# First theta stage and v's scales in another order: small operations first, an earlier table load, one sum on VectorE, mixing steps moved to the last slot

## The chip, the core and the metric

The kernel runs on one core of one Trainium2 chip. The metric is the device time of one execution in microseconds; runs are compared by their median, and one execution was taken by the hardware profiler. Times in the trace count from the start of that execution's span.

## What is computed

Windowed attention for 8 batches of 8 heads, then a block that rotates, mixes tokens and mixes channels. The reference, cut to the formulas:

```python
scores = scale * np.matmul(q, k.transpose(0, 1, 3, 2))        # 8 x 8 x 576 x 576, head size 64
mask = (rel >= 0) & (rel < 128)
scores = np.where(mask, scores + bias[None], -1e9)
attn = softmax(scores)                                        # with 1e-9 added to the sum
x = np.matmul(attn, v)                                        # to (batch, 576, 512)
theta = x @ w_theta
zr, zi = x * np.cos(theta), x * np.sin(theta)
y = einsum('ts,bsd->btd', w_tok_r, zr) + einsum('ts,bsd->btd', w_tok_i, zi)
u = x + y
return u + np.maximum(u @ w_ch, 0.0)
```

## The kernel before

The 576 tokens are five tiles, four of 128 and one of 64. Heads go in pairs, four pairs a batch. For a pair, TensorE makes the scores from `qh` and `kh` (and, from the seventh pair on, the low parts `ql` and `kl`), VectorE adds the bias and takes the row's least value (`weigh`, L552), ScalarE takes the exp (L555) into `front` and `back`. The weights are transposed, on TensorE for the early pairs (copied back as `pt`, L575), and by a DMA for the later ones, from `hl`: a cast by ScalarE (L580) and its remainder by VectorE (L583). `values` multiplies by v, `finish` (L614 to L621) writes `x_sb`.

The theta stage (`turn`) of a batch flips `x_sb` block by block on TensorE (`columns`, L655). ScalarE casts a block to `x_hi` (L665 for the short first one, L673), VectorE makes the remainder (L667, L674: `x_lo`). `products` multiplies by `wth_hi` and `wth_lo`, 8 or 12 matmuls a block; `angle` and `waves` reduce the angle and take sine and cosine on ScalarE, which needs another function table (L741 loads it); `turned` multiplies by x and the scale `zs` (L721 on VectorE) and splits the result into two f16 halves, `z_hi` (L647, ScalarE) and `z_lo` (L649, VectorE; L727 and L728 for the short block). `mix` is token mixing: nine chunks c for eight groups of outputs, three matmuls a step, with `z_hi`, `z_hi` and `z_lo`; L810 to L815 finish a group. Mixing of batch 0 is a generator whose steps are handed out while batch 1's attention runs: FIRST gives four counts for each pair.

Everything is in f16 or f32r halves with power-of-two scales, and these must be known first. In the first theta stage `scales_from` takes the largest sum over rows (`sums`, by L216 on ScalarE while the token weights are unpacked by L196, L197, L203 and L206) and over columns (`add_sizes`: TensorE sums |w| with a column of ones), `spread_from` (L315) flips and reduces a peak over partitions, and `scales_to` spreads it and makes `zs`. For v, `add_up` (L309) sums |v| over three groups of heads on ScalarE (L312), `spread_first` and `spread_scales` make its scale for batch 1's later pairs. The channel weights are unpacked one after the other (`late`, with L203, L206, L211, L212) during batch 1's attention.

The source order, `issue_after` and `high_priority` feed a scheduler that lists each engine's instructions once, before the run; each engine works through its list in order and waits at semaphores. From the first mixing matmul on, TensorE keeps the source order.

```python
FIRST = ((9, 2, 1, 7), (3, 3, 4, 3), (4, 3, 4, 2), (3, 3, 3, 0))
KEPT = 3                     # token-weight chunks that are split late: wtk_lo by L235
GROUP = 4                    # heads whose v is loaded and measured together
```

## Time and profile before

| | us |
|---|---|
| median of 3 runs (lowest, highest) | 625.47 (623.98, 626.39) |
| profiled execution | 623.47 |
| its span, first to last instruction | 621.7 |
| TensorE busy | 595.0 (96%) |
| VectorE busy | 522.5 (84%) |
| ScalarE busy | 486.6 (78%) |
| GpSimd busy | 207.9 (33%) |

In the rows, PE is TensorE's matmuls and PEld its weight loads, DVE is VectorE, ACT ScalarE, POOL GpSimd, SPq SyncE's queue of DMA issues; L12 is line 12 of the kernel before. A tile's name stands without its buffer's number. Idle time in brackets is the time just before an instruction in which its engine did nothing, with what ended it. Busy time on an engine that waits for others elsewhere says little by itself: the stage and the wait that ends last there count.

### The profile page before, as it was taken

The numbers are of one execution on the slowest core, as the hardware profiler recorded it, in microseconds if no ns is written. First come the engines' busy times: TensorE is split into PE (matmuls) and PEld (weight loads), VectorE is DVE, ScalarE is ACT, GpSimd is POOL, SyncE is SP. The second block draws the span as 40 slices with busy tenths as digits, with TensorE's granted clock in tenths as the row PEclk, the third lists the DMA queues.
The fourth block names the chain that finished last, engine by engine and source line by source line (L and its number), as shares of the span: only waits on it lengthen the run. The fifth ranks groups of instructions, "written<-read, shape, count | busy, mean of one in ns | idle before, by whom it ended". The sixth has DMA issues, their size and how long they took to land.

```text
span 621.7 us, 14873 instructions
## 1 busy us (share of the span) xinstructions
PE 595.0 (96%) x5731; PEld 488.6 (79%) x5731; DVE 522.5 (84%) x1345; ACT 486.6 (78%) x918; POOL 207.9 (33%) x261
## 2 busy tenths in 40 slices
PE   4997899889999999999999999999999999999997
PEld 3796678767888888888778878887888878887776
DVE  4889796989999889998899889997899879946733
ACT  3988899878788689887998699877998798828610
POOL 5963304440325312541225312441235221530200
PEclk9899999989999999999999999999999999999999
DMA  8971112791268901984079902994089703650001
GB/s 315 390 250 45 35 35 88 177 219 38 77 155 189 216 30 52 212 212 103 30 143 196 221 30 60 211 210 107 20 182 177 157 30 86 103 98 29 21 20 58
DMA packets 137847, 78.10 MB, mean 126 GB/s; under 512 B 110768, under 2 KB 127280, under 8 KB 137776
## 3 DMA queue, kind: packets, MB, share of 16 engines
q1 hardware_dynamic: 137776, 77.15, 51.6%
q8 instruction: 45, 0.74, 0.5%
q14 instruction: 26, 0.21, 0.1%
HBM read 40.44 MB, written 9.44 MB: 80 GB/s over the span
## 4 chain that ended last, share of the span: by engine, by line
PE 48%; DVE 26%; ACT 19%; DMA 3%; issue 3%; SPq 0%; DVEq 0%; ACTq 0%
PE mm L77 38%; PE ps L77 8%; DVE hl L583 3%; ACT front L555 2%; DVE back L552 2%; ACT back L555 2%; DVE z_lo L649 2%; DVE g L721 2%; DVE front L552 2%; PE ps L102 2%; ACT z_hi L647 1%; ACT g L712 1%; DVE f L721 1%; DVE f L702 1%; ACT g L705 1%
## 5 line engine op out<-in xcount | busy, mean ns | idle before, releaser
L77 PE MATMUL mm<-wtk_hi,z_lo 128*128 128x288 f16 x576 | 165.4, 287 | 0.7 <-DVE z_lo L649 0.6
L77 PE MATMUL mm<-wtk_hi,z_hi 128*128 128x288 f16 x576 | 165.8, 288 | 0.0
L77 PE MATMUL mm<-wtk_lo,z_hi 128*128 128x288 f16 x576 | 165.4, 287 | 0.0
L77 PEld LDWEIGHTS <-z_hi 128*128 128x128 f16 x1152 | 109.1, 98 | 29.9 <-issue 0.3
L814 POOL TENSOR_SCALAR us<-xtf,fixed 128x288 f32<-128x288 f32 x56 | 79.1, 1416 | 84.9 <-DVE xtf L810 83.4
L77 PE MATMUL mm<-u,wch_hi 128*128 128x288 f16 x512 | 81.3, 286 | 0.0
L555 ACT ACTIVATE front<-front,fixed 128x256 f32<-128x256 f32 (+2 forms) x160 | 60.1, 443 | 15.3 <-DVE fixed L552 15.1
L77 PEld LDWEIGHTS <-z_lo 128*128 128x128 f16 x576 | 56.6, 98 | 15.9 <-DVE z_lo L649 1.3
L77 PEld LDWEIGHTS <-wch_hi 128*128 128x128 f16 x512 | 48.1, 98 | 18.2 <-issue 7.1
L812 ACT ACTIVATE u<-xtf,fixed 128x288 f16<-128x288 f32 x64 | 33.5, 526 | 32.7 <-DVE xtf L810 32.6
L555 ACT ACTIVATE back<-back,fixed 128x256 f32<-128x256 f32 x128 | 56.3, 494 | 2.4 <-DVE fixed L552 2.4
L815 POOL TENSOR_TENSOR u<-us,u 128x288 f16<-128x288 f32 x56 | 41.4, 754 | 46.2 <-DVE vl L486 30.5
L649 POOL TENSOR_TENSOR z_lo<-g,z_hi 128x512 f16<-128x512 f32 x14 | 16.4, 1170 | 107.5 <-ACT z_hi L647 107.5
L77 PE MATMUL ps<-vh,pt 128*128 128x65 f16 x936 | 47.4, 194 | 3.3 <-DMA pt<-hl 3.3
L77 PE MATMUL ps<-kh,qh 64*128 64x256 f32 (+1 forms) x304 | 46.5, 344 | 4.0 <-DVE x_sb L621 2.0
L77 PEld LDWEIGHTS <-pt 128*128 128x128 f16 x1404 | 46.3, 98 | 5.0 <-DMA pt<-hl 3.8
L77 PE MATMUL mm<-wth_hi,x_hi 128*128 128x512 f32 x160 | 46.6, 413 | 2.6 <-DVE x_hi L667 2.6
L77 PE MATMUL ps<-vl,pt 128*128 128x64 f16 x468 | 45.6, 193 | 0.0
L810 DVE SCALAR_TENSOR_TENSOR xtf<-mm,fixed,xtf 128x288 f32<-128x288 f32 x64 | 32.1, 510 | 15.0 <-PE mm L77 15.0
L77 PE MATMUL mm<-wth_lo,x_hi 128*128 128x512 f32 x160 | 44.0, 395 | 0.0
L843 DVE SCALAR_TENSOR_TENSOR xtf<-mm,fixed,xtf 128x288 f32<-128x288 f32 x64 | 32.8, 513 | 12.4 <-PE mm L77 11.0
L77 PE MATMUL mm<-u,wch_lo 128*128 128x288 f16 x256 | 41.8, 286 | 0.0
(215 smaller groups left out, 1439.4 us busy)
## 6 DMA issues: line engine op xcount, KB each, us to landing
vb<-in_vx_dram SPq DMA_DIRECT2D x16, 650.0 KB, 5.3
out_dram<-xtf SPq DMA_DIRECT2D x64, 144.0 KB, 1.7
qr<-in_qk_dram SPq DMA_DIRECT2D x26, 320.0 KB, 3.1
kr<-in_qk_dram SPq DMA_DIRECT2D x26, 288.0 KB, 4.2
xtf<-in_wch_dram SPq DMA_DIRECT2D x4, 512.0 KB, 3.5
qh<-in_qk_dram SPq DMA_DIRECT2D x6, 320.0 KB, 6.1
kh<-in_qk_dram SPq DMA_DIRECT2D x6, 288.0 KB, 6.4
xtf<-in_wtok_dram SPq DMA_DIRECT2D x3, 576.0 KB, 9.8
```

The lines of the kernel that those rows point to most:

```text
L77: ins = nc.tensor.matmul(*args, **kw)
L102: ins = nc.tensor.transpose(*args)
L552: self.weighed = nc.vector.tensor_tensor_reduce(out=sb, in0=ps, in1=bias, scale=self.scale, scalar=3.0e38, op0=ALU.add, op1=ALU.min, accum ...
L555: self.exps.append(nc.scalar.activation(sb, sb, AF.Exp, bias=least, scale=-1.0))
L583: self.lowered = nc.vector.scalar_tensor_tensor(out=hl[:, 1], in0=src, scalar=2.0 ** PEXP, in1=hl[:, 0], op0=ALU.mult, op1=ALU.subtract)
L649: low = engine.tensor_tensor(out=z_lo[:, c, :], in0=z, in1=z_hi[:, c, :], op=ALU.subtract)
L721: nc.vector.scalar_tensor_tensor(out=z, in0=x_sb[:, i, :], scalar=zs[:, c:c + 1], in1=z, op0=ALU.mult, op1=ALU.mult)
L810: nc.vector.scalar_tensor_tensor(out=xtf[:, m, cs], in0=y_ps[:, :HALF], scalar=st["back"], in1=xtf[:, m, cs], op0=ALU.mult, op1=ALU.add)
L812: nc.scalar.activation(u_hi[:, m, cs], xtf[:, m, cs], AF.Copy, scale=up)
L814: nc.gpsimd.tensor_scalar(out=us[:, m, cs], in0=xtf[:, m, cs], scalar1=up, scalar2=None, op0=ALU.mult)
L815: lows.append(lambda m=m, cs=cs: nc.gpsimd.tensor_tensor(out=u_lo[:, m, cs], in0=us[:, m, cs], in1=u_hi[:, m, cs], op=ALU.subtract))
L843: nc.vector.scalar_tensor_tensor(out=xtf[:, e, cs], in0=o_ps[:, :HALF], scalar=down, in1=xtf[:, e, cs], op0=ALU.mult, op1=ALU.max)
```

## The change

In the first theta stage `add_sizes` gets a first matmul with a small constant (`least`), which stands for the 1.0 that L423 added; the sums of the second half are made before the second block's products; the three parts of the scale chain are placed between the products of blocks 1, 2 and 3 in the source (`late`, `place`), and `x_lo`, L725 and L726 come after the bound. The table load (`early`) waits for the attention's exps and `x_hi` alone. The last token weights are unpacked in another order (`lift`, HOLD), and the three late splits follow the bound. `turned` runs for four blocks at once (`j >= 3`). For v, `largest` takes the third group's largest |v| on VectorE in place of a sum on ScalarE, `spread_first` and `spread_scales` stand half a pair earlier. FIRST gives the first pair two steps less and the last pair five more; three fewer run after it.

```diff
-FIRST = ((9, 2, 1, 7), (3, 3, 4, 3), (4, 3, 4, 2), (3, 3, 3, 0))
+HOLD = 2
+
+FIRST = ((9, 2, 1, 5), (3, 3, 4, 3), (4, 3, 4, 2), (3, 4, 7, 0))
...
+        def lift(k, t):
+            if k in lifted:
+                return
+            lifted.append(k)
+            _, z, b = words(k, t)
+            nc.vector.scalar_tensor_tensor(out=b, in0=z, scalar=3, in1=b, op0=ALU.logical_shift_left,
+                                           op1=ALU.bitwise_or)
+
         def together(k, t):
             raw, z, b = words(k, t)
             val = b.bitcast(F32)
-            nc.vector.scalar_tensor_tensor(out=b, in0=z, scalar=3, in1=b, op0=ALU.logical_shift_left,
-                                           op1=ALU.bitwise_or)
+            lift(k, t)
...
-            for stage, fn in ((3, split), (2, together), (1, apart)):
+            for stage, fn in ((3, split), (2, together), (1, apart)) if k != n else ((1, apart), (2, together)):
                 j = k - stage
+                if j == n - 2 and stage == 2:
+                    lift(j, tiles[j])
+                    yield HOLD
                 if 0 <= j < n and (stage < 3 or j < n - KEPT):
                     if j not in tiles:
                         tiles[j] = load(j)
                     fn(j, tiles[j])
                     if stage == 3:
                         del tiles[j]
-                    if stage == 1 and j > 0:
+                    if k == n and stage == 2:
+                        row(j)
+                    elif stage == 1 and 0 < j < n - 1:
                         row(j - 1)
...
+    def largest(g, to):
+
+        nc.vector.tensor_reduce(out=to, in_=group_v[g].rearrange("p h c d -> p (h c) d")[:, :, :64],
+                                axis=mybir.AxisListType.XY, op=ALU.max, apply_absolute_value=True)
...
         if start:
             size_ps.append(ps_m.tile([128, 512], F32, name="mm")[:, :HALF])
+            mm(size_ps[hf], one.broadcast_to([128, 128]), least.broadcast_to([128, HALF]), start=True, stop=False)
         for c in some:
-            mm(size_ps[hf], one.broadcast_to([128, 128]), sizes[c][:, hf * HALF:hf * HALF + HALF],
-               start=(start and c == some[0]), stop=(stop and c == some[-1]))
+            mm(size_ps[hf], one.broadcast_to([128, 128]), sizes[c][:, hf * HALF:hf * HALF + HALF], start=False,
+               stop=(stop and c == some[-1]))
...
                                 op0=ALU.mult, op1=ALU.max)
-        add_sizes(1, ORDER[:7], True, False)
         for hf in range(2):
-            add_sizes(hf, ORDER[7:], False, True)
+            add_sizes(hf, ORDER[8:], False, True)
             nc.vector.tensor_reduce(out=lim if hf else peak[:, 3:4], in_=size_ps[hf], axis=mybir.AxisListType.X,
                                     op=ALU.max)
-        nc.vector.tensor_scalar(out=peak[:, 3:4], in0=peak[:, 3:4], scalar1=lim, scalar2=2.0 ** (WEXP - 1),
-                                op0=ALU.max, op1=ALU.mult)
-        nc.vector.tensor_scalar(out=peak[:, 3:4], in0=peak[:, 3:4], scalar1=1.0, scalar2=None, op0=ALU.add)
+        return nc.vector.tensor_scalar(out=peak[:, 3:4], in0=peak[:, 3:4], scalar1=lim, scalar2=2.0 ** (WEXP - 1),
+                                       op0=ALU.max, op1=ALU.mult)
...
+            with tc.issue_after(st["bound"].ins) if "bound" in st else nullcontext():
+                st["rest"] = nc.vector.tensor_tensor(out=x_lo, in0=x_ps, in1=x_hi.bitcast(F32), op=ALU.subtract)
...
-        def products(t_ps, x_hi, x_lo):
+        def products(t_ps, x_hi, x_lo, late=None):
             prods = ((x_hi, wth_hi), (x_hi, wth_lo)) + (((x_lo, wth_hi),) if x_lo is not None else ())
             for k, (a, w) in enumerate(prods):
                 for c in range(4):
+                    if late is not None and (k, c) == late[0]:
+                        late[1]()
...
+                with nullcontext() if st["b"] else tc.issue_after(st["bound"].ins):
+                    nc.vector.tensor_tensor(out=g[:64], in0=x_sb[:64, i, :], in1=g[:64], op=ALU.mult)
+                    nc.vector.tensor_tensor(out=g[64:], in0=x_sb[:64, i, :], in1=f[:64], op=ALU.mult)
...
-            if not st["b"]:
-                early(st["exps"] + [st["kept"], row_sums[-1]])
...
                 if not st["b"] and j == 0:
+                    early(st["exps"] + [st["lifted"]])
                     with tc.issue_after(st["flipped"].ins):
                         add_sizes(0, ORDER[:7], True, False)
                 for k, g in enumerate(coming(st["b"])):
                     if j == k and st["b"]:
                         with tc.issue_after(st["rest"].ins):
                             measure(g, peaks[st["b"] % 2][:, GROUP * k:GROUP * k + GROUP])
-                ready.append(theta(i, cur))
+                def between_products():
+                    with tc.issue_after(st["angled"].ins), tc.high_priority(FINISH):
+                        if j == 1:
+                            st["bound"] = scales_from()
+                        elif j == 2:
+                            st["diag"] = spread_from(peaks[0], 4, "0")
+                        else:
+                            scales_to(st["diag"])
+
+                place = {1: (2, 0), 2: (1, 0), 3: (1, 0)}.get(j) if not st["b"] else None
+                ready.append(theta(i, cur, place and (place, between_products)))
                 if st["b"] != 1:
                     waves(*ready[-1])
                 elif j > 2:
                     for some in ready:
                         waves(*some)
-                if j < 3 and not st["b"]:
+                if j == 0 and not st["b"]:
                     with tc.issue_after(st["angled"].ins), tc.high_priority(FINISH):
-                        if j == 0:
-                            scales_from()
-                        elif j == 1:
-                            diag = spread_from(peaks[0], 4, "0")
-                        else:
-                            scales_to(diag)
-                if j >= (2, 3, 0)[min(st["b"], 2)]:
+                        add_sizes(1, ORDER[:8], True, False)
+                        add_sizes(0, ORDER[7:8], False, False)
+                if j >= (3, 3, 0)[min(st["b"], 2)]:
                     for some in ready:
                         turned(*some)
...
             step(mixing, steps[1])
-            if g == (b == 1):
+            if g == 0 and b > 1:
                 diag = spread_first(b - 1)
+            if b == 1 and g == 1:
+                spread_scales(0, diag)
             step(mixing, steps[2])
+            if b == 1 and g == 0:
+                with tc.issue_after(new.weighed.ins):
+                    largest(2, peaks[0][:, 2:3])
             pair.values()
             with tc.high_priority(FINISH):
                 done = pair.finish(x_sb)
-                if b == 1 and g == 1:
-                    spread_scales(0, diag)
             if new is not None and (new.early or g == 0):
...
                     with behind_all(new.exps):
-                        for k, g_v in enumerate(coming(0)):
+                        for k, g_v in enumerate(coming(0)[:2]):
                             add_up(g_v, peaks[0][:, k:k + 1])
...
 
     def start(x_sb, load):
...
-            with behind_all([st[0]["split"], st[0]["kept"]]):
+            with behind_all([st[0]["split"]]), tc.high_priority(FINISH):
                 while next(kept, False):
...
-    with tc.issue_after(done.ins):
-        for _ in kept:
-            pass
+    for k in range(KEPT):
+        with behind_all([done, st[0]["bound"]]):
+            next(kept, None)
...
-                    step(mixing, 6)
+                    step(mixing, 3)
```

Where it moves instructions, first on VectorE at the beginning of the first theta stage, from the end of the first batch's attention on. Before:

```order
L621 TENSOR_TENSOR x_sb<-ps,fixed 128x2x5x64
L203 SCALAR_TENSOR_TENSOR us<-us 128x576
L203 SCALAR_TENSOR_TENSOR xtf<-xtf 128x576
L235 SCALAR_TENSOR_TENSOR wtk_lo<-u,fixed,wtk_hi 128x576
L206 SCALAR_TENSOR_TENSOR us<-us 128x576
L667 TENSOR_TENSOR x_hi<-ps,x_hi 128x4x64
L206 SCALAR_TENSOR_TENSOR xtf<-xtf 128x576
L674 TENSOR_TENSOR x_lo<-ps,x_hi 128x512
```

With the change, whose lines are numbered anew (L209 was L203, L217 was L206, L246 was L235, L687 was L667, L695 was L674):

```order
L641 TENSOR_TENSOR x_sb<-ps,fixed 128x2x5x64
L209 SCALAR_TENSOR_TENSOR us<-us 128x576
L687 TENSOR_TENSOR x_hi<-ps,x_hi 128x4x64
L217 SCALAR_TENSOR_TENSOR us<-us 128x576
L209 SCALAR_TENSOR_TENSOR xtf<-xtf 128x576
L695 TENSOR_TENSOR x_lo<-ps,x_hi 128x512
L217 SCALAR_TENSOR_TENSOR xtf<-xtf 128x576
```

The low half of `x_hi` stands behind one of the four unpacking operations; the L235 of `u` comes some fifteen instructions later.

Then VectorE where z is made, at the end of the same stage. Before:

```order
L721 SCALAR_TENSOR_TENSOR g<-x_sb,fixed,g 128x512
L721 SCALAR_TENSOR_TENSOR f<-x_sb,fixed,f 128x512
L721 SCALAR_TENSOR_TENSOR wch<-x_sb,fixed,wch 128x512 x2
L728 SCALAR_TENSOR_TENSOR z_lo<-g,fixed,z_hi 128x512
L702 SCALAR_TENSOR_TENSOR wch<-wch,mm 128x512
L649 TENSOR_TENSOR z_lo<-g,z_hi 128x512
L649 TENSOR_TENSOR z_lo<-f,z_hi 128x512
L649 TENSOR_TENSOR z_lo<-wch,z_hi 128x512 x2
L702 SCALAR_TENSOR_TENSOR wch_lo<-wch_lo,mm 128x512
L721 SCALAR_TENSOR_TENSOR wch<-x_sb,fixed,wch 128x512 x2
L649 TENSOR_TENSOR z_lo<-wch,z_hi 128x512
L721 SCALAR_TENSOR_TENSOR wch_lo<-x_sb,fixed,wch_lo 128x512 x2
```

With the change (L745 was L721, L753 was L728, L726 was L702, L669 was L649):

```order
L745 SCALAR_TENSOR_TENSOR g<-x_sb,fixed,g 128x512
L745 SCALAR_TENSOR_TENSOR f<-x_sb,fixed,f 128x512
L745 SCALAR_TENSOR_TENSOR wch<-x_sb,fixed,wch 128x512 x2
L753 SCALAR_TENSOR_TENSOR z_lo<-g,fixed,z_hi 128x512
L745 SCALAR_TENSOR_TENSOR wch<-x_sb,fixed,wch 128x512 x2
L726 SCALAR_TENSOR_TENSOR wch_lo<-wch_lo,mm 128x512
L669 TENSOR_TENSOR z_lo<-g,z_hi 128x512
L669 TENSOR_TENSOR z_lo<-f,z_hi 128x512
L669 TENSOR_TENSOR z_lo<-wch,z_hi 128x512 x4
L745 SCALAR_TENSOR_TENSOR wch_lo<-x_sb,fixed,wch_lo 128x512 x2
L669 TENSOR_TENSOR z_lo<-wch_lo,z_hi 128x512 x2
```

The multiplications of all blocks but the last now stand ahead of the first remainder `z_lo`.

Last, ScalarE at the end of batch 1's attention, up to the second theta stage. Before:

```order
L484 ACTIVATE vh<-vb,fixed 128x5x64
L812 ACTIVATE u<-xtf,fixed 128x288
L580 ACTIVATE hl<-back 128x1024
L484 ACTIVATE vh<-vb,fixed 128x5x64
L456 ACTIVATE qh<-qr 128x640
L457 CAST kh<-kr 128x576
L665 CAST x_hi<-ps 128x4x64
L673 CAST x_hi<-ps 128x512
L812 ACTIVATE u<-xtf,fixed 128x288
```

With the change (L842 was L812, L600 was L580, L476 and L477 were L456 and L457, L504 was L484, L685 and L693 were L665 and L673):

```order
L842 ACTIVATE u<-xtf,fixed 128x288
L600 ACTIVATE hl<-back 128x1024
L476 ACTIVATE qh<-qr 128x640
L504 ACTIVATE vh<-vb,fixed 128x5x64
L477 CAST kh<-kr 128x576
L504 ACTIVATE vh<-vb,fixed 128x5x64
L842 ACTIVATE u<-xtf,fixed 128x288
L685 CAST x_hi<-ps 128x4x64
L693 CAST x_hi<-ps 128x512
```

One `vh` and one `u` now stand between `kh` and `x_hi`.

## Rows read from the trace of the kernel before

**Rows 1.** Busy time by stage: us, busy (instructions) of each engine, TensorE's clock, DMA.
```profile
107.00:122.00 15.00, 13.28 (x124) 11.61 (x122) 14.89 (x49) 12.61 (x28) 7.26 (x10) 1.00 0.78 190
...
140.00:152.00 12.00, 11.53 (x58) 9.52 (x59) 11.25 (x20) 10.09 (x16) 1.39 (x4) 1.00 0.20 46
```
**Rows 2.** TensorE's timeline: start us, us, instruction, idle time before and its end.
```profile
61.75 1.21 PE L77 MATMUL mm<-wth_hi,x_hi 128*128 128x512 f32 x4 [1.44 <-DVE x_hi L667]
...
70.85 0.30 PE L102 MATMUL mm<-fixed,peak 128*128 128x128 f32 x1 [1.91 <-ACT xtf L676]
...
81.50 0.30 PE L77 MATMUL mm<-wtk_hi,z_lo 128*128 128x288 f16 x1 [0.65 <-DVE z_lo L649]
...
105.47 0.39 PE L77 MATMUL ps<-kh,qh 64*128 64x256 f32 x2 [0.80 <-ACT pt L575]
...
114.92 0.38 PE L77 MATMUL mm<-fixed 128*128 128x3 f32 x2 [1.72 <-DVE fixed L321]
...
130.70 0.20 PE L77 MATMUL ps<-vh,pt 128*128 128x65 f16 x1 [0.51 <-DMA pt<-hl]
...
133.10 0.20 PE L77 MATMUL ps<-vh,pt 128*128 128x65 f16 x1 [1.87 <-DMA pt<-hl]
...
140.47 1.20 PE L77 MATMUL mm<-wth_hi,x_hi 128*128 128x512 f32 x4 [1.18 <-DVE x_hi L667]
```
**Rows 3.** The chain that ended last, just before the second theta stage: start us, us, what.
```profile
132.74 6.26 DMA kr<-in_qk_dram
...
139.02 0.67 ACT kh L457
```
**Rows 4.** VectorE's timeline, as rows 2.
```profile
61.27 0.42 DVE L667 TENSOR_TENSOR x_hi<-ps,x_hi 128x256 fp32r<-128x256 f32 x1
...
76.84 0.75 DVE L721 SCALAR_TENSOR_TENSOR g<-x_sb,fixed,g 128x512 f32<-128x512 f32 x1
...
80.76 0.68 DVE L649 TENSOR_TENSOR z_lo<-g,z_hi 128x512 f16<-128x512 f32 x1
...
98.02 0.17 DVE L614 TENSOR_SCALAR fixed<-ps 128x10 f32<-128x10 f32 x1 [1.60 <-PE ps L77]
...
111.47 0.28 DVE L319 TENSOR_REDUCE fixed<-mm 128x1 f32<-128x128 f32 x1
...
114.40 0.46 DVE L321 TENSOR_SCALAR fixed<-fixed 128x3 f32<-128x3 f32 x1
```
**Rows 5.** ScalarE's timeline, as rows 2.
```profile
59.05 0.37 ACT L665 CAST x_hi<-ps 128x256 fp32r<-128x256 f32 x1 [0.34 <-PE ps L102]
...
61.39 0.69 ACT L216 ACTIVATE wch<-us 128x576 bf16<-128x576 f32 x1 [1.32 <-DVE us L206]
...
63.19 1.28 ACT L741 ACT_TABLE_LOAD   x1
64.48 0.20 ACT L741 ACTIVATE scratch<-fixed 128x1 f32<-128x1 f32 x1
...
101.40 1.27 ACT L312 ACTIVATE wch_lo<-vb 128x1280 f16<-128x1280 f32 x1
...
134.24 0.52 ACT L812 ACTIVATE u<-xtf,fixed 128x288 f16<-128x288 f32 x1
...
135.62 0.55 ACT L484 ACTIVATE vh<-vb,fixed 128x320 f16<-128x320 f32 x1
```
**Rows 6.** Busy time by stretch, as rows 1; the eighth figure is TensorE's granted clock.
```profile
15.00:21.00 6.00, 5.30 (x22) 3.51 (x23) 5.96 (x20) 5.32 (x13) 5.78 (x5) 0.50 1.04 381
69.00:71.00 2.00, 0.15 (x2) 0.18 (x3) 1.97 (x6) 2.00 (x5) 0.00 (x0) 1.00 0.12 12
130.90:134.30 3.40, 1.53 (x51) 1.41 (x48) 3.37 (x8) 3.10 (x8) 0.50 (x2) 1.00 0.96 202
134.30:137.70 3.40, 3.40 (x23) 2.19 (x20) 2.94 (x6) 2.45 (x5) 1.54 (x3) 0.50 1.50 317
```
**Rows 7.** DMA issues of the whole span: count, KB each, median us to landing.
```profile
kr<-in_qk_dram SPq DMA_DIRECT2D x26, 288.0 KB, 4.2
```

More of the change, by code (lines that the diff above doesn't have):

```diff
@@ L127, in attn_moe_kernel @@
     scratch = const.tile([128, 1], F32, name="scratch")
-    one = const.tile([128, 1], BF16, name="one")
+    one, least = (const.tile([128, 1], BF16, name=name) for name in ("one", "least"))
     bands = const.tile([128, 704], F32, name="bands")
@@ L135, in attn_moe_kernel @@
     nc.vector.memset(one, 1.0)
+    nc.gpsimd.memset(least, 2.0 ** -(WEXP + 6))
     wth_hi = const.tile([128, 4, DM], F32R, name="wth_hi")
@@ L198, in apart @@
                                     scalar2=-0.5 + 7.5 * 2.0 ** -19, op0=ALU.mult, op1=ALU.add)
+        lifted = []
+        def lift(k, t):
[5 more added lines that the diff above has]
+                                           op1=ALU.bitwise_or)
         def together(k, t):
@@ L673, in columns @@
                 st["lifted"] = nc.scalar.copy(x_hi, x_ps)
-            st["rest"] = nc.vector.tensor_tensor(out=x_lo, in0=x_ps, in1=x_hi.bitcast(F32), op=ALU.subtract)
+            with tc.issue_after(st["bound"].ins) if "bound" in st else nullcontext():
+                st["rest"] = nc.vector.tensor_tensor(out=x_lo, in0=x_ps, in1=x_hi.bitcast(F32), op=ALU.subtract)
             keep = nc.vector.tensor_copy if st["b"] and i > 2 else nc.scalar.copy
@@ L697, in angle @@
                 th = f[:64]
-                nc.scalar.copy(g[:64], t_ps[64:])
+                with nullcontext() if st["b"] else tc.high_priority(FINISH):
+                    nc.scalar.copy(g[:64], t_ps[64:])
                 nc.vector.tensor_tensor(out=th, in0=t_ps[:64], in1=g[:64], op=ALU.add)
@@ L724, in turned @@
             else:
-                nc.vector.tensor_tensor(out=g[:64], in0=x_sb[:64, i, :], in1=g[:64], op=ALU.mult)
-                nc.vector.tensor_tensor(out=g[64:], in0=x_sb[:64, i, :], in1=f[:64], op=ALU.mult)
+                with nullcontext() if st["b"] else tc.issue_after(st["bound"].ins):
+                    nc.vector.tensor_tensor(out=g[:64], in0=x_sb[:64, i, :], in1=g[:64], op=ALU.mult)
+                    nc.vector.tensor_tensor(out=g[64:], in0=x_sb[:64, i, :], in1=f[:64], op=ALU.mult)
                 nc.scalar.activation(z_hi[:, 8, :], g, AF.Copy, scale=zs[:, 8:9])
@@ L729, in turned, with theta @@
                                                op0=ALU.mult, op1=ALU.subtract)
-        def theta(i, parts):
+        def theta(i, parts, late=None):
             t_ps = ps_m.tile([128, 512], F32, name="mm")
-            products(t_ps, *parts)
+            products(t_ps, *parts, late)
             return angle(i, t_ps)
@@ L932, in attend @@
                             step(late)
+                if b == 1 and g == 0:
+                    diag = spread_first(0)
             else:
@@ L945, in start @@
     def start(x_sb, load):
-        paces = [0]
+        paces, held = [0], []
         def pace(new, k):
@@ L952, in pace @@
                     paces[0] += 1
-                    if paces[0] * 7 % 10 < 7:
-                        next(load, None)
+                    if paces[0] * 7 % 10 < 7 and not held and next(load, None) == HOLD:
+                        held.append(True)
         prepare(0)
```

## The prediction

> **What bounds the kernel now.** The order of the instructions comes first: but for a memset, the two programs do the same in the same order on every engine up to the first theta stage, and again from the second theta stage's first matmul on, save one swap on ScalarE. What differs lies between 57 and 141 us of the span. The first view is therefore the busy time by stage [rows 1]. From 140 us on TensorE is the bound, 11.53 of 12.00 us busy; ahead of it VectorE is (14.89 of 15.00 us from 107 to 122, TensorE only 13.28). The second view is what TensorE waits for in this part [rows 2]: 1.44 us for `x_hi`, 1.91 before the peak's flip, 0.65 for a `z_lo`, 0.80 for a `pt` copy, 1.72 for L321, 0.51 and 1.87 for the DMA transposes, 1.18 for the second stage's `x_hi`. These eight, 10.1 us, are the most that can be won. The third view is the chain of work just before the second theta stage [rows 3]: the `kr` load is issued at 132.74, when VectorE has done with its buffer, and takes 6.26 us; `kh` on ScalarE waits for it until 139.02; `x_hi` stands behind `kh` in ScalarE's queue, and the first matmul of the second theta stage, 140.47 [rows 2], behind `x_hi`. **The change is worth what it moves that matmul by**, and what TensorE's clock does around it.
>
> **The change, part by part.** Times are on the profiled execution's scale.
>
> *Small operations in front.* The low half of `x_hi` stood on VectorE behind two L203, an L235 and an L206 and began at 61.27 [rows 4]. Now one L203 is ahead of it, and ScalarE's half, done at 59.05 + 0.37 = 59.42 [rows 5], ends its wait. It is ready near 59.9. TensorE then still has eight sums of 288 columns in front (`least` and seven), 0.12 us each at 2.4 GHz, so theta's products start near 60.3 instead of 61.75: 1.4 us sooner. The 1.91 us before the peak's flip go too, since the third block's products now stand ahead of the flip. Part of both comes back, because the diagonal's matmul is now behind the fourth block's products and L321 behind all three L235: I take theta's last product 2 us earlier, near 78 (it would be 3.3 if nothing came back).
>
> *The table load sooner.* It takes 1.28 us and now falls into the 1.32 us that ScalarE waited for L206 [rows 5]. It costs nothing there; without that cover it would cost 1.28. The Trainium skill (ScalarE: Activation LUTs, What ACT_TABLE_LOAD costs) adds a drain of 1.38 us to a load, 2.66 in all, which would overrun the gap by 1.3. The trace does not bear it out: the next instruction starts at 64.48, 1.29 after the load's start [rows 5].
>
> *All four blocks' z at once.* This is the term that speaks against the change. From the first L721 (76.84) to the first L649 (80.76) VectorE does six operations, four L721, one L728 and one L702: 3.92 us, 0.65 each [rows 4]. Now two more L721 stand in front, 1.3 us. And the chain of scales that L721 waits for is not shorter: what it wins at its start it loses behind the L235 and an L702. I take it 0.3 later, so the first L649 starts at 76.84 + 0.3 + 5.2 = 82.4, not 80.76. TensorE waited for this `z_lo` at 81.50 [rows 2] and ran freely 0.6 later, from 82.1; now from 83.75, **1.65 us later**, after an idle stretch of over 5 us that begins near 78. Bounds: 1.3 (chain unmoved) and 2.1.
>
> *One of three sums on VectorE.* An L312 of 1.27 us [rows 5] leaves ScalarE. Of the maximum that replaces it no row shows the form: L319 does 128x128 in 0.28 us [rows 4], L312 the same 1280 elements in 1.27. It is nearest to the second; I take 1.3. VectorE waited 1.60 us for the values just there [rows 4], so it is free; without that wait it costs 1.3. ScalarE's 1.27 I count at nothing: it now waits for the last block's z near 86, and the `pt` copies and an L212 that filled this stand behind, ahead of the exp table. The other end is all of the 1.27.
>
> *TensorE up to the wait for `pt`.* It is 1.65 late, does two mixing steps less (three matmuls of 288 columns each, 0.36, so 0.72) and no longer waits 0.80 for `pt` [rows 2]. That leaves 0.1 late at the matmuls of 105.47, and VectorE, which weighs them, goes on where it did.
>
> *The wait for L321.* TensorE loses its 1.72 us, but VectorE is full there, and only VectorE's own saving moves the end: L319 and L321, 0.28 and 0.46 [rows 4], are done earlier in idle time. Of these 0.74 ScalarE gives most back, since an L212 and a third exp of `back` now stand before the `hl` cast that VectorE waits for next. I keep 0.15 at the issue of `kr`; the ends are 0 and 0.74.
>
> *Steps to the last slot.* Five steps, 1.8 us, go before the last values, into the 2.38 us that TensorE waited for transposes [rows 2]; three come out of the tail. Both ends lie under the `kr` chain, so I count nothing. Without that cover they are worth up to 1.8.
>
> *Behind `kh`.* Before, ScalarE did `u` (0.52, at 134.24) and the second `vh` (0.55, at 135.62) ahead of `kh` [rows 5], while it waited for loads anyway. Now both stand between `kh` and `x_hi`: 1.07, less about 0.1 of overlap each, so 0.9 on the path.
>
> *The rest.* One memset on GpSimd at the start and an L423 less on VectorE: nothing. SyncE's order of DMAs is unchanged; its second transposes, `vb` and `kr` each move with the VectorE operation that frees them. GpSimd's moved L211 and `us` are waited for by nobody on this chain.
>
> **Sum.** 0.9 - 0.15 = **+0.75 us**. The profiled execution took 623.47 us (span 621.7, 1.8 around it), so 624.2. The median of the runs shown, 625.47, is 2.0 above that execution; on its scale the forecast is **626.2 us**. A difference below 0.5%, 3.1 us, is about what a measurement of this kernel can't tell from none.
>
> **The rivals.**
> *Slower: the clock falls at the handover.* TensorE would idle over 5 us before 83.75 with some five matmuls in it. The trace shows the clock at 0.50 right after a stretch with 1.53 us busy in 3.40, and at 1.00 in one with 0.15 in 2.00 [rows 6], so a short gap decides nothing, but this one is longer than both. The fall then lasted 3.4 us, and near the start it covers all of 15 to 21 [rows 6]. At 1.2 GHz for 3.4 us TensorE loses 1.7 us; passed on in full that is +0.75 + 1.7 = +2.45, still no change. At half for 6.8 us it loses 3.4: +4.15, **629.6 us**. It decides beyond 2 x (3.1 - 0.75) = 4.7 us at the low clock. By the Trainium skill (TensorE: Matmul & The Clock Gate, Part 1: The HAM clock gate) the slow clock is the default and only activity lifts it; by that rule a fall here is near certain, which the 69 to 71 row alone would not make it.
> *Faster: ScalarE's lead is kept.* If its 1.27 and VectorE's 0.74 us both reach `kr`, that load is issued 2.0 us sooner, clear of the `vb` load ahead of it, and may land in 4.2 us, the median of its 26 [rows 7], not 6.26: 2.0 + 2.06 - 0.9 = 3.2 us, **622.3 us**. For it: ScalarE has no idle time left in that part. Against it: the z order holds TensorE back whatever ScalarE does.
> *Nothing is moved.* Lead and loss cancel under the `kr` chain: 625.5 us.
>
> **How the numbers follow.** The forecast with the case of no move and the short fall of the clock, all within 3.1 us of before: 0.60. The long fall, slower: 0.22. The kept lead, faster: 0.18. By the bounds of its terms the likeliest case alone reaches from 624.3 (1.27 and the rest of the 0.74 won as well) to 628.5 (nothing won, z at its late bound, the short fall of the clock: 0.15 + 0.45 + 1.7 more). The range that holds 8 in 10 reaches into both rivals: from 622.3 to 629.3.
>
> **What would show it.** In the profile after: theta's first product near 60.3; an idle stretch of TensorE before 84 of 4 us or more that ends with L649's line, the first of which starts near 82.4; no wait at 115 for the v diagonal; the waits for transposes shorter by 1 to 2 us; `kr` issued near 132.6, and `kh`, `vh`, `u`, `x_hi` in this order until the matmul near 141.2. A granted clock of 0.5 between 81 and 90 points to the first rival. The forecast is wrong if the second theta stage begins before 138 or after 144.

## The result, and the profile after

The changed kernel takes 629.77 us (median of 14 runs, 627.04 to 632.49) against 625.91 of the kernel before in the same runs (14, 623.98 to 629.95): the ratio is 1.0054, with a 95% interval from 1.0032 to 1.0076. It is slower by about 3.4 us: its interval excludes a ratio of 1, but the difference is hardly more than the 0.5% that the forecast took for what can be told. On the scale of the forecast, 625.47 x 1.0054 = 628.8: inside the range, 2.6 above the value that was forecast, and 0.8 below the figure of the slower rival. The profiled execution took 631.62 us (span 629.8), 1.9 above its median, while that of before was 2.4 below its own. So 8.1 us lie between the two spans, and not all of them belong to the change.

TensorE's timeline after the change, columns as in [rows 2]; L103 flips, L78 is every other matmul:

```profile
60.45 0.77 PE L103 MATMUL ps<-fixed,x_sb 128*128 128x128 f32 x5 [1.04 <-DVE x_sb L641]
...
61.94 1.20 PE L78 MATMUL mm<-wth_hi,x_hi 128*128 128x512 f32 x4
...
82.36 0.30 PE L78 MATMUL mm<-wtk_hi,z_lo 128*128 128x288 f16 x1 [2.10 <-DVE z_lo L753]
...
84.88 0.42 PE L78 MATMUL mm<-wtk_hi,z_lo 128*128 128x288 f16 x1 [1.82 <-DVE z_lo L669]
85.09 0.45 PE L78 MATMUL mm<-wtk_hi,z_hi 128*128 128x288 f16 x1
85.33 0.45 PE L78 MATMUL mm<-wtk_lo,z_hi 128*128 128x288 f16 x1
...
95.95 0.49 PE L78 MATMUL mm<-kh,qh 128*128 128x192 f32 x2
...
141.24 0.77 PE L103 MATMUL ps<-fixed,x_sb 128*128 128x128 f32 x5 [1.58 <-DVE x_sb L641]
144.70 2.08 PE L78 MATMUL mm<-wth_hi,x_hi 128*128 128x512 f32 x4 [2.70 <-DVE x_hi L687]
```

And of the kernel before, where the last flips of the first theta stage begin, and the next scores:

```profile
58.68 0.77 PE L102 MATMUL ps<-fixed,x_sb 128*128 128x128 f32 x5 [1.04 <-DVE x_sb L621]
...
90.60 0.49 PE L77 MATMUL mm<-kh,qh 128*128 128x192 f32 x2
```

The last flips start 1.77 us later than before. Nothing shows that the change does this: in the traces of the kernels below that were made from the changed one they start anywhere from 58.47 to 60.75, in those made from the kernel before from 58.96 to 59.28. From here on times are therefore counted from these flips.

Busy time by stretch, after; the eighth figure is TensorE's granted clock (1.00 is 2.4 GHz, 0.50 is 1.2 GHz):

```profile
79.80:82.40 2.60, 0.47 (x4) 0.16 (x4) 2.60 (x5) 2.60 (x6) 0.67 (x1) 1.00 0.00 0
82.60:89.40 6.80, 4.98 (x22) 2.79 (x20) 6.78 (x12) 4.50 (x9) 0.00 (x0) 0.50 0.01 2
107.00:122.00 15.00, 15.00 (x149) 13.12 (x147) 13.18 (x40) 14.01 (x29) 8.85 (x14) 1.00 0.55 133
134.00:138.00 4.00, 4.00 (x74) 3.51 (x72) 3.96 (x10) 4.00 (x10) 1.07 (x1) 1.00 0.94 185
144.00:150.60 6.60, 5.90 (x16) 4.77 (x17) 3.94 (x7) 3.17 (x7) 1.43 (x2) 0.50 0.25 56
```

Two rows at 0.50 are new. The first is at the handover, where TensorE goes from the first theta stage to the mixing and waits for z. From 82.6 to 89.4 the mixing matmuls follow each other every 0.24 us (85.09, 85.33) where they take 0.12 at 1.00: from 84.88 to 89.41 that is 19 of them, 4.53 us in place of 2.32, **2.2 us lost**. From 144.0 to 150.6 the clock is low again, and the second theta stage's products, which begin at 144.70, run at half speed: the first twelve and what stands between them take 6.28 us (to 150.98) where before they took 3.47 (140.47 to 143.94), about **2.8 us lost**. Before, the clock was low from 134.3 to 137.7 [rows 6], ahead of that stage, where TensorE had only the wait for `kr` behind it. The stretch from 107 to 122 is now TensorE's, 15.00 of 15.00 us; before it was VectorE's [rows 1].

VectorE's timeline, and then the chain that ended last, after, as [rows 3, 4]:

```profile
78.89 0.75 DVE L745 SCALAR_TENSOR_TENSOR g<-x_sb,fixed,g 128x512 f32<-128x512 f32 x1
...
84.15 0.68 DVE L669 TENSOR_TENSOR z_lo<-g,z_hi 128x512 f16<-128x512 f32 x1
...
101.25 1.48 DVE L327 TENSOR_REDUCE peak<-vb 128x1 f32<-128x1280 f32 x1
```

```profile
136.43 5.92 DMA kr<-in_qk_dram
142.35 0.02 issue
142.37 0.67 ACT kh L477
143.04 0.46 ACT vh L504
143.50 0.42 ACT u L842
143.93 0.27 ACT x_hi L685
```

Counted from the flips, in us (each is a row's start less that of the flips):

| | theta's products | first `z_lo` of four | next scores | `kr` issued | `kh` | second theta stage | from there to the end |
|---|---|---|---|---|---|---|---|
| before | 3.07 | 22.08 | 31.92 | 74.06 | 80.34 | 81.79 | 481.2 |
| after | 1.49 | 23.70 | 35.50 | 75.98 | 81.92 | 84.25 | 485.1 |

So the second theta stage starts 2.46 us later and the rest takes 3.9 more, of which the low clock explains 2.8. With the 1.77 ahead of the flips this is the difference of the spans. The table also says where 2.46 comes from: 3.58 late at the scores (1.4 by VectorE's order, 2.2 by the clock), 1.66 won back up to `kr`, 0.34 by a quicker landing, and 0.88 lost between `kh` and the first product.

### The profile page after: what moved, and what is told of

Same layout as the page of the kernel before. It is cut to its first block, busy times and chain, and to the rows that moved or that the text cites. A ratio compares the mean times of both kernels' runs of the same rounds, so it can differ in the third digit from the quotient of the medians.

```text
span 629.8 us, 14876 instructions
## 1 busy us (share of the span) xinstructions
PE 601.7 (96%) x5733; PEld 492.6 (78%) x5733; DVE 525.0 (83%) x1345; ACT 484.7 (77%) x916; POOL 208.8 (33%) x262
## 4 chain that ended last, share of the span: by engine, by line
PE 53%; DVE 24%; ACT 14%; DMA 5%; issue 3%; SPq 0%; POOL 0%; DVEq 0%; ACTq 0%; POOLq 0%
PE mm L78 41%; PE ps L78 10%; DVE hl L603 2%; PE ps L103 2%; ACT back L575 2%; DMA pt<-hl 2%; DVE front L572 2%; ACT hl L600 2%; DVE g L745 1%; ACT front L575 1%; DVE f L745 1%; DVE back L572 1%; DVE z_lo L669 1%; ACT g L736 1%; DVE f L726 1%
## 5 line engine op out<-in xcount | busy, mean ns | idle before, releaser
L78 PE MATMUL mm<-wtk_hi,z_lo 128*128 128x288 f16 x576 | 165.8, 288 | 3.9 <-DVE z_lo L753 2.1
L78 PE MATMUL mm<-wtk_hi,z_hi 128*128 128x288 f16 x576 | 166.1, 288 | 0.0
L78 PE MATMUL mm<-wtk_lo,z_hi 128*128 128x288 f16 x576 | 165.9, 288 | 0.0
L78 PEld LDWEIGHTS <-z_hi 128*128 128x128 f16 x1152 | 109.3, 99 | 30.3 <-ACT z_hi L752 0.5
L844 POOL TENSOR_SCALAR us<-xtf,fixed 128x288 f32<-128x288 f32 x56 | 80.8, 1446 | 96.9 <-DVE xtf L840 96.1
L78 PE MATMUL mm<-u,wch_hi 128*128 128x288 f16 x512 | 81.3, 286 | 0.0
L78 PEld LDWEIGHTS <-z_lo 128*128 128x128 f16 x576 | 56.6, 98 | 19.4 <-DVE z_lo L669 2.5
L78 PEld LDWEIGHTS <-wch_hi 128*128 128x128 f16 x512 | 48.1, 98 | 18.2 <-issue 7.1
L842 ACT ACTIVATE u<-xtf,fixed 128x288 f16<-128x288 f32 x64 | 33.6, 526 | 33.8 <-DVE xtf L840 33.7
L845 POOL TENSOR_TENSOR u<-us,u 128x288 f16<-128x288 f32 x56 | 40.5, 738 | 42.7 <-DVE vl L506 18.5
L669 POOL TENSOR_TENSOR z_lo<-g,z_hi 128x512 f16<-128x512 f32 x14 | 16.4, 1169 | 107.4 <-ACT z_hi L667 107.4
L78 PE MATMUL ps<-kh,qh 64*128 64x256 f32 (+1 forms) x304 | 46.7, 346 | 5.3 <-DVE x_sb L641 4.2
L78 PE MATMUL mm<-wth_hi,x_hi 128*128 128x512 f32 x160 | 48.6, 426 | 2.7 <-DVE x_hi L687 2.7
L78 PEld LDWEIGHTS <-pt 128*128 128x128 f16 x1404 | 46.2, 98 | 3.6 <-DMA pt<-hl 2.0
L78 PE MATMUL ps<-vh,pt 128*128 128x65 f16 x936 | 47.3, 194 | 1.8 <-DMA pt<-hl 1.7
L78 PE MATMUL ps<-vl,pt 128*128 128x64 f16 x468 | 45.6, 193 | 0.0
L78 PE MATMUL mm<-wth_lo,x_hi 128*128 128x512 f32 x160 | 44.7, 402 | 0.0
L78 PE MATMUL mm<-u,wch_lo 128*128 128x288 f16 x256 | 41.8, 286 | 0.0
## 6 DMA issues: line engine op xcount, KB each, us to landing
out_dram<-xtf SPq DMA_DIRECT2D x64, 144.0 KB, 1.8
```

Source lines behind the costliest of these rows:

```text
L78: ins = nc.tensor.matmul(*args, **kw)
L669: low = engine.tensor_tensor(out=z_lo[:, c, :], in0=z, in1=z_hi[:, c, :], op=ALU.subtract)
L842: nc.scalar.activation(u_hi[:, m, cs], xtf[:, m, cs], AF.Copy, scale=up)
L844: nc.gpsimd.tensor_scalar(out=us[:, m, cs], in0=xtf[:, m, cs], scalar1=up, scalar2=None, op0=ALU.mult)
L845: lows.append(lambda m=m, cs=cs: nc.gpsimd.tensor_tensor(out=u_lo[:, m, cs], in0=us[:, m, cs], in1=u_hi[:, m, cs], op=ALU.subtract))
```

## Experiments

The mean granted clock over all runs is a second reading beside the time: 0.984 for the changed kernel, 0.988 to 0.989 for the kernel before in each of the three groups that were run together (first to fourth, fifth to eighth, ninth to twelfth kernel below). It does not rank kernels by itself: e7 has 0.992 at a ratio of 1.0001. A ratio is always to the kernel before in the same group, so ratios of different groups can be set side by side, times can't.

### e1_z_three: the fourth block's z behind the first three

```diff
-                    for some in ready:
-                        turned(*some)
+                    for n, some in enumerate(ready):
+                        with tc.issue_after(st["lowered"].ins) if n == 3 > st["b"] * 4 else nullcontext(): turned(*some)
```

> The changed kernel, with the fourth block's z put behind the remainders of the first three on VectorE, as before the change; nothing else moves on any engine but ScalarE's matching z_hi. Theory A (the z order and the tail both cost, each by a delay and by TensorE's clock): the first L669 starts about 1.3 us sooner than the 84.15 of the changed kernel, counted from theta's first product 20.9 us behind it instead of 22.2; no granted clock of 0.5 between that handover and the next scores; the second theta stage starts 1.5 to 2 us sooner; ratio to the kernel before 1.002 to 1.003. Rival B (only the tail costs, what is lost at the handover is made up before the second theta stage): 1.0045 to 1.006. Rival C (only the handover costs, the late tail follows from it): 1.000 or below.

Measured: 625.55 us, ratio 1.0001 (0.9978 to 1.0023), mean clock 0.989. The loss is gone, as far as the interval tells. TensorE and its clock in this kernel:

```profile
81.86 0.30 PE L78 MATMUL mm<-wtk_hi,z_lo 128*128 128x288 f16 x1 [2.03 <-DVE z_lo L753]
...
83.06 0.30 PE L78 MATMUL mm<-wtk_hi,z_lo 128*128 128x288 f16 x1 [0.66 <-DVE z_lo L669]
```

```profile
82.00:90.00 8.00, 7.28 (x60) 5.75 (x59) 8.00 (x14) 7.17 (x13) 0.00 (x0) 1.00 0.06 12
128.00:133.00 5.00, 5.00 (x34) 3.31 (x31) 5.00 (x23) 4.90 (x13) 1.42 (x2) 0.66 0.96 175
```

The second of the two waits is 0.66 in place of 1.82, and no 0.50 follows it; the low clock of this trace lies from 128.6 to 132.0 instead. The second theta stage starts 79.89 behind the flips, 4.4 sooner than in the changed kernel, where theory A had 1.5 to 2. By the time, rival C comes nearest; but the edit takes away the delay and the fall together, so it can't say which of them cost.

### e2_steps_old, e3_z_and_steps, e4_steps_alone: the steps

```diff
-FIRST = ((9, 2, 1, 5), (3, 3, 4, 3), (4, 3, 4, 2), (3, 4, 7, 0))
+FIRST = ((9, 2, 1, 7), (3, 3, 4, 3), (4, 3, 4, 2), (3, 3, 3, 0))
-                    step(mixing, 3)
+                    step(mixing, 6)
```

This edit in the changed kernel; with that of e1 in the second; and its reverse in the kernel before in the third.

> The changed kernel with the old counts of mixing steps (two more for the first pair, five fewer for the last, three more in the tail); ScalarE's order at the end of batch 1's attention goes back with it, vh and u ahead of kh. Theory A: TensorE waits for the transposes again and its clock may fall there, under cover; the second theta stage runs at 1.0 and starts about 0.85 us sooner behind the landing of kr; the 0.5 at the handover of the first stage stays: 3 to 4 us less than the changed kernel, ratio 0.999 to 1.001. Rival B: the same, 0.998 to 1.000. Rival C: still 1.004 to 1.006.

> Both of the former edits in the changed kernel: z of three blocks first, and the old counts of mixing steps. Theory A: both falls of the clock gone, the 1.4 us won at theta's start kept in part: 2 us below the kernel with the old steps alone, ratio 0.995 to 0.998. Rival B: as with the old steps alone, 0.998 to 1.000. Rival C: as with the z order alone, about 1.000.

> The kernel before with the new counts of mixing steps alone (two less for the first pair, five more for the last, three less in the tail). Theories A and B: the waits for the transposes are filled, TensorE idles ahead of the second theta stage instead, and its clock is at 0.5 in the stage's first 6 to 7 us: 3 to 4 us more, ratio 1.004 to 1.006. Rival C: the steps are covered either way, 0.999 to 1.001.

Measured: 628.07 us, 1.0034 (1.0016 to 1.0052); 627.02, 1.0020 (1.0000 to 1.0039); 626.80, 1.0017 (0.9999 to 1.0035). By the medians A and B missed all three. C is nearest each time, though a little off, and its values lie within or touch each interval. The mechanism that A and B named is there to see in the third kernel: with the waits for the transposes filled, TensorE idles just ahead of the second theta stage, and the clock is low in that stage instead of before it:

```profile
134.00:138.00 4.00, 2.99 (x50) 2.50 (x45) 3.88 (x7) 3.00 (x5) 1.91 (x3) 1.00 1.37 326
138.00:141.00 3.00, 0.28 (x3) 0.10 (x1) 1.23 (x4) 1.56 (x4) 1.71 (x2) 0.76 0.83 178
141.00:146.00 5.00, 5.00 (x15) 4.02 (x16) 3.03 (x5) 1.90 (x5) 0.74 (x1) 0.50 0.34 78
```

But over the runs it costs 1.1 us, not 3 to 4, and the interval reaches down to no cost at all. And with the old steps the changed kernel stays slow: in its trace the clock was at 0.50 again at the handover, and again at the transposes, this time for seven microseconds:

```profile
85.00:89.00 4.00, 3.88 (x18) 2.28 (x19) 4.00 (x8) 1.77 (x4) 0.00 (x0) 0.57 0.02 4
...
136.50:143.50 7.00, 5.72 (x57) 4.50 (x58) 5.57 (x10) 5.15 (x10) 2.03 (x4) 0.51 1.21 250
```

### e5_fill: the wait filled, the order kept

The one that tells delay and clock apart. Matmuls of constants, as the kernel already has them elsewhere, into a buffer of the scores' pool that nobody reads:

```diff
+GROUP, FILL = 4, (16, 14)
...
+    def fill(n):
+
+        ps = ps_s.tile([128, 2, 512], F32, name="ps")[:, 0]
+        flat = ident.bitcast(BF16)
+        for _ in range(n):
+            mm(ps[:, :256], flat[:, :128], flat, start=True, stop=True)
...
                 for n, (z, w) in enumerate(((z_hi, wtk_hi), (z_hi, wtk_lo), (z_lo, wtk_hi))):
+                    if st["b"] == g == 0 and k < 2 and n == 2:
+                        fill(FILL[k])
```

> The changed kernel with its four-blocks-first z, and with matmuls of constants, whose result nobody reads, put on TensorE into its two waits at the handover: 16 of 128x256 ahead of the first z_lo, 14 ahead of the second. VectorE's order is as in the changed kernel, so the first L669 still comes 23.7 us behind the last flips' start. Theory A1 (most of what the z order costs is the clock that falls in the wait): no granted clock of 0.5 between 80 and 92, the next scores about 2.2 us sooner, ratio to the kernel before 1.001 to 1.003. Rival A2 (the cost is VectorE's lateness by itself): the clock stays up, but the time does not follow, 1.004 to 1.006. Rival A3 (the clock falls for another reason than TensorE's idleness): still 0.5 there, 1.004 to 1.006.

Measured: 625.35 us, ratio **0.9976** (0.9953 to 0.9999), mean clock 0.991. Against 1.0054 that is 4.9 us for thirty matmuls that nobody reads, more than A1 asked for.

```profile
78.69 1.91 PE L78 MATMUL ps<-fixed 128*128 128x256 bf16 x16
80.95 0.30 PE L78 MATMUL mm<-wtk_hi,z_lo 128*128 128x288 f16 x1 [0.34 <-DVE z_lo L760]
...
81.33 1.69 PE L78 MATMUL ps<-fixed 128*128 128x256 bf16 x14
83.47 0.30 PE L78 MATMUL mm<-wtk_hi,z_lo 128*128 128x288 f16 x1 [0.45 <-DVE z_lo L676]
```

```profile
81.00:90.00 9.00, 8.48 (x71) 6.84 (x71) 8.24 (x14) 6.75 (x13) 0.00 (x0) 1.00 0.00 0
127.00:132.00 5.00, 4.31 (x28) 3.30 (x29) 5.00 (x23) 3.85 (x10) 2.12 (x3) 0.66 1.07 180
```

The flips, the next scores, the issue of `kr` and the second theta stage of this kernel, and VectorE's first `z_lo` of four:

```profile
59.06 0.77 PE L110 MATMUL ps<-fixed,x_sb 128*128 128x128 f32 x5 [1.03 <-DVE x_sb L648]
...
82.74 0.68 DVE L676 TENSOR_TENSOR z_lo<-g,z_hi 128x512 f16<-128x512 f32 x1
...
92.57 0.49 PE L78 MATMUL mm<-kh,qh 128*128 128x192 f32 x2
...
132.67 0.33 SPq L310 DMA_DIRECT2D kr<-in_qk_dram  x1
...
140.25 1.20 PE L78 MATMUL mm<-wth_hi,x_hi 128*128 128x512 f32 x4 [0.82 <-DVE x_hi L694]
```

VectorE is as late as in the changed kernel (its first `z_lo` of four 23.68 behind the flips, there 23.70), but TensorE goes on at 1.00: the scores come 33.51 behind the flips, not 35.50, and the second theta stage 81.19, not 84.25. A2 and A3 fall. That stage runs at 1.00 too, though nothing was filled there: the clock falls from 127.6 to 131.0 in this trace, behind a wait of 2.34 us for `x_sb` that the changed kernel has as well (131.46) without a fall. So the fill removes the loss, but which part of the 4.9 us comes from the handover itself and which from the second stage's clock, this run doesn't tell.

### e6_v_old, e7_v_alone: v's scales

The part on v undone in the kernel of e1 (three `add_up`, no `largest`, `spread_first` and `spread_scales` at their old places), and that part alone in the kernel before:

```diff
             step(mixing, steps[1])
-            if g == 0 and b > 1:
+            if g == (b == 1):
                 diag = spread_first(b - 1)
-            if b == 1 and g == 1:
-                spread_scales(0, diag)
             step(mixing, steps[2])
-            if b == 1 and g == 0:
-                with tc.issue_after(new.weighed.ins):
-                    largest(2, peaks[0][:, 2:3])
             pair.values()
             with tc.high_priority(FINISH):
                 done = pair.finish(x_sb)
+                if b == 1 and g == 1:
+                    spread_scales(0, diag)
...
-                        for k, g_v in enumerate(coming(0)[:2]):
+                        for k, g_v in enumerate(coming(0)):
...
-                if b == 1 and g == 0:
-                    diag = spread_first(0)
```

> The changed kernel with z of three blocks first and with v's scale chain as before: three sums on ScalarE, no maximum on VectorE, spread_first and spread_scales at their old places. The new counts of mixing steps stay. If the part on v wins what the kernel with three blocks first has over the one before it undone (TensorE's wait for L321 and ScalarE's sum), this is 1 to 2 us slower than that kernel, ratio 1.002 to 1.003. If the part on v is worth nothing: 0.999 to 1.001. If it costs: below 0.998.

> The kernel before with the new chain of v's scales alone. If TensorE's 1.72 us at L321 and ScalarE's 1.27 reach the second theta stage: 1.5 to 2.5 us less, ratio 0.996 to 0.998. If VectorE's load sets that stage and keeps them: 0.999 to 1.001. If the new order of ScalarE behind it (u and vh against kh) costs: 1.001 to 1.003.

Measured: 627.72 us, 1.0021 (1.0000 to 1.0042), and 625.92 us, 1.0001 (0.9980 to 1.0022). Alone the part wins nothing; taken out of the kernel of e1 it costs 1.2 us, which these intervals don't resolve. The traces say more. From the next scores to the issue of `kr` it is 42.1 us in the kernel before, 42.3 in e4 (the steps alone), 42.8 in e7 (v alone), 42.2 in e6 and 41.7 and 42.1 in e2 and e3 (one of the two missing in each), but 40.5 in the changed kernel, 40.4 in e1 and 40.1 in e5, which have both. In e4 and e7 (the first two and the last two lines):

```profile
91.11 0.49 PE L77 MATMUL mm<-kh,qh 128*128 128x192 f32 x2
133.40 0.33 SPq L287 DMA_DIRECT2D kr<-in_qk_dram  x1
...
91.19 0.49 PE L77 MATMUL mm<-kh,qh 128*128 128x192 f32 x2
133.97 0.33 SPq L287 DMA_DIRECT2D kr<-in_qk_dram  x1
```

**The two parts win 1.7 us there together and nothing, or at most 0.4 (e2), singly,** by one trace of each kernel. Why is open: each edit also makes the scheduler list ScalarE's and VectorE's operations of that part anew, and no run took the steps and these lists apart.

### e8_z_fill, e9_before_fill: the better order with its wait filled, and a control

e1 and e5 together, with 14 and 4 matmuls; and five in the 0.65 us that the kernel before waits at its handover.

> The changed kernel with z of three blocks first and the matmuls of constants in the handover, 14 ahead of the first z_lo and 4 ahead of the second. If the clock at the handover, of which the one profile of the kernel without them shows no fall, still falls in part of its runs: mean granted clock over the runs higher by 0.001 to 0.003, ratio 0.997 to 0.999. If it does not: as without them, 0.999 to 1.001.

> The kernel before with five matmuls of constants in its own wait of 0.65 us at the handover, ahead of the second z_lo; nothing else moves. A control for the two kernels with such matmuls. If what those won over the kernel before belongs to the change with its wait filled: 0.999 to 1.001 here, since the kernel before shows no granted clock of 0.5 at its handover. If it belongs to the matmuls alone, whatever the order: 0.996 to 0.998.

Measured: 624.07 us, ratio **0.9965** (0.9945 to 0.9986), and 627.12 us, ratio 1.0007 (0.9981 to 1.0032). Five such matmuls show no gain in the kernel before, whose trace has no 0.50 at the handover. In the kernel of e1 they win 0.36%, barely resolved, for the intervals overlap from 0.9978 to 0.9986. That fits e3 and e6: with the same order and the same first wait (2.03 and 2.04) they do show 0.50 for 3.4 us at the handover, though the one trace of e1 does not. That the clock fell there in a part of the runs of e1 isn't shown. Against e5 the better order is worth 0.1%, 0.7 us, not resolved.

### e10_two_fills, e11_x_hi_vector, e12_all: the second theta stage

To the kernel of e8 are added matmuls of constants in the two waits ahead of the second theta stage (`fill` then takes the pool of its buffer as an argument); or the short block's `x_hi` by VectorE; or both (then 18 and 6 matmuls at the handover, 12 and 4 ahead of the stage).

```diff
+GROUP, FILL, SECOND = 4, (14, 4), (12, 14)
...
             for c in range(4):
+                if st["b"] == 1 and i == 0 and c == 3:
+                    fill(SECOND[0], ps_m)
                 st["flipped"] = flipped(x_ps[:, c * n:c * n + 128], x_sb[:, i, c * 128:c * 128 + 128], ident)
...
+                if st["b"] == 1 and j == 0:
+                    fill(SECOND[1], ps_m)
                 ready.append(theta(i, cur, place and (place, between_products)))
...
-                nc.scalar.copy(both[:, :, 0], x_ps)
+                (nc.vector.tensor_copy if st["b"] == 1 else nc.scalar.copy)(both[:, :, 0], x_ps)
```

> The changed kernel with z of three blocks first, with the matmuls of constants at the handover (14 and 4), and with 12 and 14 more in TensorE's two waits ahead of the second theta stage: before the flips that wait for the last x_sb, and behind them. If that stage loses time to the clock in a part of the runs (its first 3.4 us at 0.5 in the one profile without them): 1 to 2 us less than that kernel, ratio 0.993 to 0.996, and no 0.5 between 138 and 150. If the clock then falls elsewhere or the stage does not set the end: as without them, 0.996 to 0.998.

> The changed kernel with z of three blocks first and with the matmuls of constants at the handover, and with the second theta stage's first x_hi, of the short block, made by VectorE in place of ScalarE. So it no longer stands behind kh, the second vh and u. VectorE waits there. If that queue is what holds the second stage's first matmul: it starts 0.7 to 1 us sooner against the issue of kr (7.2 us behind it in the kernel without this, so about 6.3), ratio 0.995. If the second block's x_hi, still on ScalarE behind them, or the clock takes it back: as without, 0.9965.

> All of it: z of three blocks first, matmuls of constants at the handover (18 and 6) and ahead of the second theta stage (12 and 4), the short block's x_hi by VectorE. If each of these does what it should, ratio 0.992 to 0.995 against the kernel before; if the waits overlap, as the better of the two kernels with one of them, 0.995 to 0.9965.

Measured: 622.55 us, ratio **0.9940** (0.9920 to 0.9961), mean clock 0.993; 622.64 us, 0.9939 (0.9915 to 0.9964), 0.991; 622.89 us, 0.9937 (0.9911 to 0.9964), 0.992. All three are faster than both kernels; against e8, measured in another group, the intervals overlap. In the first the stage runs at full clock from its start:

```profile
134.00:138.00 4.00, 3.77 (x35) 3.18 (x33) 3.46 (x7) 2.04 (x4) 1.39 (x4) 1.00 1.12 226
138.00:150.00 12.00, 11.44 (x62) 9.32 (x60) 10.26 (x19) 9.76 (x18) 1.99 (x4) 1.00 0.27 52
```

The second did not do what it was to do. The stage's first product comes 8.36 us behind the issue of `kr`, not 6.3 (e8: 7.21), for the chain now runs through VectorE's own queue, where two `vl` stand ahead:

```profile
136.29 0.82 DVE x_sb L648
137.11 1.40 DVE vl L513 x2
138.51 0.34 DVE x_hi L692
```

Its time against e8 (0.9939 and 0.9965, in different groups, intervals overlapping) is thus not explained by that queue; in its trace the clock fell at 127.3 instead, ahead of the idle time before that stage. The third lies in the range that was expected if each part did its work, but so do the first two without the other's part: that they add up isn't seen.

## Why the prediction was right or wrong

The time lies in the forecast's range, but the likeliest case isn't what took place: the clock fell at the handover, as the slower rival said. By the letter of its last sign the forecast would be wrong: the second theta stage begins at 144.70, behind 144. Less the 1.77 us that the trace was late at the flips it is 142.93, inside.

**Small operations in front: right.** Theta's products start 1.58 us sooner against the flips (1.4 forecast), the last of its product groups 2.2 sooner (2 forecast).

**The table load: right.** It runs from 61.86, takes 1.28, and the next instruction starts 1.30 after it:

```profile
61.86 1.28 ACT L766 ACT_TABLE_LOAD   x1
63.16 0.20 ACT L766 ACTIVATE scratch<-fixed 128x1 f32<-128x1 f32 x1
```

**All four blocks' z at once: the delay right, its price not.** The first L745 came 0.28 us later (0.3 forecast), the first `z_lo` of four 1.62 (1.65 forecast). The idle time was not one stretch of over 5 us but two waits, 2.10 and 1.82, with three matmuls between. But the forecast of the likeliest case stopped at the delay, with a short fall of the clock as its late bound. What took place is the mechanism of the slower rival, which had 0.22: 0.50 for 6.8 us at the handover. Its place and length were as it said; its chance was too small. Its price was not: TensorE was busy for 4.98 of the 6.80 us, so 2.2 us were lost there and not 3.4, and the second theta stage starts 2.46 later and not 4.15. That the time comes so near to the rival's (628.8 and 629.6 on the same scale) is partly luck: a second fall, at the start of the second theta stage, which no rival had, added some 2.8. e5 shows that the clock, and not the delay, made the change slow: with the delay kept and the clock held at the handover, the same kernel is at 0.9976. By the rule of the Trainium skill that the forecast weighed (TensorE: Matmul & The Clock Gate, Part 1: The HAM clock gate), only activity lifts the slow clock. The fall in the trace and e5, where matmuls in the waits keep it off, agree. That a fall here is near certain the runs do not bear out: behind a first wait of 2.03 to 2.04 us it came in e3 and e6, not in e1. So the single row at 69 to 71 us [rows 6], a wait of 1.91 us without a fall, told little either way.

**One of three sums on VectorE: nearly.** The maximum takes 1.48 us (1.3 forecast), and L321's wait on TensorE is gone as forecast.

**The wait for L321 and the steps to the last slot: wrong.** The forecast kept 0.15 us at the issue of `kr` for the first and counted nothing for the second. The traces show 1.7 us, but only where both are in (e4, e6 and e7 have one each). "Both ends lie under the `kr` chain" also missed what the steps do to the clock: they take the idle time, and with it the low clock, from under the cover of 134 to 138 us [rows 6] to the front of the second theta stage (the trace of e4; over its runs a cost isn't resolved).

**Behind `kh`: right.** The second `vh` (0.46) and `u` (0.42) now stand there. From the start of `kh` to the first product 1.45 us became 2.33: 0.88 (0.9 forecast).

**The sum.** The forecast +0.75 us stood for the second stage's start; the profile has +2.46 there, and some 2.8 of low clock behind it. With the clock held at the handover (e5) the start is 0.6 us earlier than before. So without the fall at the handover the walk through the order was 1.35 us too pessimistic, about as much as the 1.7 us up to `kr` exceed the 0.15 that was counted for them, and with the fall it was too optimistic. The rival that nothing moves falls with the table: the second theta stage starts 2.46 later. The rival of ScalarE's kept lead did not come either: `kr` is issued 1.92 later against the flips, not 2.0 sooner, and takes 5.92 us to land, not 4.2.

## What to carry to other kernels

In this kernel a wait on TensorE had two prices: its length, and what the granted clock did behind it. So read the clock in the stretch after each wait that an edit makes longer, in more than one trace, and try a few matmuls of constants in the wait before the order is blamed. What a low clock costs depends on where it falls. In the kernel before it lay from 134.3 to 137.7, and TensorE still had 1.18 us to wait for `x_hi` behind it; with the waits ahead of it filled (e4) it lay on the stage that sets the end. And parts of a reordering can pay only together, as the steps and v's scales do here up to the issue of `kr`, so an experiment on one of them alone can show nothing.

## What was not expected of the hardware

The same order with the same first wait (2.03 us in e1 and e3, 2.04 in e6) showed no low clock at the handover in one trace (e1) and 3.4 us of it in the two others. The clock's falls also lie differently from trace to trace between 14 and 30 us, where no edit reaches, and e2 has none there. With one trace a kernel, the mean clock over a group of runs (0.984 for the changed kernel, 0.991 with its waits filled) is the better witness, though no more than a second one beside the time.
